# Two attention and two feed-forward layers: VectorE copies both single scores of a cycle, one exponential for the pair, another order of tokens in turned chunks

## The chip, the cores and the metric

The kernel runs on one core of one Trainium2 chip. The metric is the device time of one execution in microseconds (us). The engines are named as the profile names them: PE (TensorE, matmuls), DVE (VectorE), ACT (ScalarE), POOL (GpSimd) and SP (SyncE, which here only issues DMAs).

## The reference

Input x has 2048 tokens of D = 448 numbers. The same attention and the same feed-forward block are applied twice, in turn:

```python
def _A_ref(x, wq, wk, wv, wo):          # H = 16 heads of Dh = 28, one k and one v for all heads
    q = (x @ wq).reshape(B, S, H, Dh).transpose(0, 2, 1, 3)
    k = x @ wk
    v = x @ wv
    scores = jnp.einsum("bhqd,bkd->bhqk", q, k) * (Dh ** -0.5)
    p = _softmax(scores, axis=-1)
    o = jnp.einsum("bhqk,bkd->bhqd", p, v)
    return o.transpose(0, 2, 1, 3).reshape(B, S, H * Dh) @ wo
def _B_ref(x, w_gate, w_up, w_down):    # F = 1792
    return (_silu(x @ w_gate) * (x @ w_up)) @ w_down

x = x + _A_ref(_layernorm(x)); x = x + _B_ref(_layernorm(x))
x = x + _A_ref(_layernorm(x)); x = x + _B_ref(_layernorm(x))
```

All is float32. The kernel splits a float32 factor into a high and a low part and adds three products, so that PE can take the faster form of matmul; P-V alone is done in plain float32.

## The kernel before, in words

The tokens stand in four chunks of 512. The order of the instructions on each engine is the order in which the program text issues them.

**Attention (`scores`).** There are 16 groups, each of one chunk of queries and four heads. For a group the 2048 keys come in 16 tiles of 128, and a cycle (`cycle`, L610) takes two of these tiles: 16 / 2 = 8 cycles a group, 128 a layer. For each tile `tile_scores` (L592) makes four banks of scores, one a head: three lie side by side in a tile named three, the fourth, the single, in a bank of its own. In a cycle ACT makes four exponentials: of the first single out of its bank (L614), of the first three (L615), of the second three (L618), and of the second single (L619), which DVE has copied from its bank into SBUF (L617). Then PE does P-V of the cycle before (`pv`, L651) into the bank that held the first single, and DVE adds the result to the group's sum (L660). Small work of DVE, POOL and SP (`due`, `aside`) is issued behind that: the end of a group's normalisation, and the layer norm and turning of finished chunks. In the fifth cycle of some groups `outproj` (L577) multiplies a finished chunk by wo.

PE takes its work in this order: scores of two tiles for cycle m, P-V of cycle m - 1, scores for m + 1, and so on. There are eight banks: two times three, and the two of the singles, which change places from cycle to cycle. The second single of a cycle goes into the bank from which the sum of the P-V before was read.

**Turning.** Matmuls need a chunk with features on the partitions. Chunks 0 to 2 of each feed-forward layer are turned while attention runs: `turn_tile` (L266) transposes 128 tokens in blocks of 32x32 on DVE (L268) and sends them with four DMAs to a DRAM tensor (L271); later `rows3` (L130, L132) reads the whole chunk back as features by tokens, and `halved` splits it. For layer 1's attention `hand_over` (L844) makes the layer norm of a chunk as soon as the feed-forward layer has finished it, and PE turns it with 16 transposes (`flip`, L248); ACT (L254, L258) and DVE (L255, L264) take the result out of PSUM.

**Feed-forward (`unit`).** A unit is one chunk times 128 of the 1792 hidden columns. PE does the first half of gate and up (22 matmuls), one half of the unit before's down projection (12), the second half (20) and the other half of down (12). ACT reads one column of the banks ("seen", L325), for which the next half waits; then come Silu (L922), the product with up on DVE (L923), and the split into h high (ACT, L924) and low (DVE, L927). Two stage copies (L829) and POOL additions (L830) end a chunk. What `hand_over` puts into the list `soon` is issued at the end of a later unit; the number says how many units later. `project` (L298) is the q, k, v product for 112 + 16 columns of a chunk; `q` stores it to DRAM (qd, kt). When the queries of chunk 0 are stored, `fetch` (L444) loads them again, POOL casts them (L446), and `maxima` (L424) makes the shifts for the exponentials from them.

Of the kernel before, what the change touches and what calls it, by code (L numbers as in the profile page):

```python
# [55 lines left out]
def forward(  # L56
# [209 lines left out]
    def turn_tile(got, tb, raw, t):  # L266

        nc.vector.transpose(tb[:, t, :], got["x"][:, t, 0:D])  # L268
        to = raw.rearrange("(b d) (t g w) -> t g d b w", d=32, g=4, w=32)
        for g in range(4):  # L270
            nc.sync.dma_start(to[t, g], tb[32 * g : 32 * g + 32, t, :].rearrange("d (b w) -> d b w", w=32))  # L271
# [57 lines left out]
    class Attention:  # L329


        def __init__(self, layer):
            self.layer = layer
            self.X, self.norms, self.qd = {}, {}, {}
# [172 lines left out]
        def q(self, c, m):  # L507
            cs = slice(512 * c, 512 * c + 512)
            held, po = bank((3, 4, 5) if self.seen > len(self.order) - 4 else wide[-1], True)
# [9 lines left out]
            if not full and (c or not self.layer):  # L519
                if self.seen % 2 == 0:  # L520
                    self.two = wpool.tile([P, 2, 512], F32R, tag="wgh", name="q2", bufs=FG + 1)
                self.hi[m] = self.two[0:112, self.seen % 2, :]
                nc.scalar.copy(self.hi[m], po[0:112, :])
            nc.scalar.copy(raw, po)
# [7 lines left out]
            vt = vt.rearrange("p (t u d) -> p u t d", t=4, u=4)  # L532
# [21 lines left out]
        def scores(self, ff, xb):  # L554
            next(switch)
            inner = ExitStack()
            with tc.tile_pool(name=f"ow{self.layer}", bufs=1, side="right", reuse_waits="tile") as ow:
                wp = inner.enter_context(tc.tile_pool(name=f"at{self.layer}", bufs=1, reuse_waits="tile"))
                woh = ow.tile([P, NG, D], F32R, name="woh")
# [25 lines left out]
                def tile_scores(n, three, one):  # L585

                    i, kt = divmod(n, NT)
                    q, k, ks = qts[i % 3], keys[kt // 4], slice(P * (kt % 4), P * (kt % 4) + P)
                    for z, (kp, part) in enumerate(((0, 0), (1, 0), (0, 1))):
                        for j in range(4):  # L590
                            js = slice(32 * j, 32 * j + 32)
                            nc.tensor.matmul(  # L592
                                three[:, j, :] if j < 3 else one, k[js, kp, ks], q[js, part, :],
                                start=(z == 0), stop=(z == 2), tile_position=(32 * j, 0),
                            )
                    pt, pt1 = bufs[n % 4]
# [4 lines left out]
                bufs = [  # L601
                    (wp.tile([P, 3, 512], F32, name=f"pt{y}"), wp.tile([P, 512], F32, name=f"single{y}"))
                    for y in range(4)
                ]
# [5 lines left out]
                def cycle(m):  # L610

                    a, b = singles(m)
                    pt, pt1 = tile_scores(2 * m, threes[0], a)
                    es = [nc.scalar.activation(pt1, a, AF.Exp, scale=SCALE)]  # L614
                    es.append(nc.scalar.activation(pt, threes[0], AF.Exp, scale=SCALE))  # L615
                    pt, pt1 = tile_scores(2 * m + 1, threes[1], b)
                    copy = nc.vector.tensor_copy(pt1, b)  # L617
                    es.append(nc.scalar.activation(pt, threes[1], AF.Exp, scale=SCALE))  # L618
                    es.append(nc.scalar.activation(pt1, pt1, AF.Exp, scale=SCALE))  # L619
# [3 lines left out]
                    if m > 1:  # L623
                        tc.declare_no_dep(copy.ins, exps[m - 2][3], reason="P-V, which read it, waited for that")
# [20 lines left out]
                def pv(m, to):  # L645
# [18 lines left out]
                    if m + 1 in exps:  # L664
                        tc.declare_no_dep(f.ins, exps[m + 1][0], reason="P-V waited for the bank's exponential")
# [37 lines left out]
                def turns(c, got):  # L703

                    at_ = {}

                    def one(t):
                        if t == 0:
                            at_["tb"] = wp.tile([P, 4, D], F32, name="tb")
                        turn_tile(got, at_["tb"], ff.raw[c], t)  # L710
# [26 lines left out]
                for m in range(last):  # L737
# [13 lines left out]
                    cycle(m)  # L751
                    if m:
# [29 lines left out]
    class FeedForward:  # L782
# [61 lines left out]
        def hand_over(self, c):  # L844

            a = self.nxt
            fs, got = norm_steps(c)
# [3 lines left out]
            a.X[c] = xtile((xpool, self.x1p, self.xbp, self.xbp)[c])  # L851

            def ready():
                for f in fs[5:]:
                    f()
                if c > 1:
                    a.norms[c] = got

            if c == NC - 1:
                a.plan[8, 0] = [ready]  # L860
# [27 lines left out]
        def unit(self, gi, c, n):  # L888
# [33 lines left out]
            nc.scalar.activation(sg, pg[0], AF.Silu)  # L922
            nc.vector.tensor_tensor(sg, pg[1], sg, ALU.mult)  # L923
# [147 lines left out]
```

## Time and profile before

| | |
|---|---|
| median of 3 runs | 1992.53 us (1992.45 to 1994.26) |
| the profiled execution | 1995.44 us |
| its span, first to last instruction | 1993.7 us |
| mean granted TensorE clock | 0.997 |
| busy: PE / ACT / DVE / POOL | 1973.1 / 1276.1 / 782.7 / 559.9 us |
| attention of layer 0 and of layer 1 | about 69 to 577 us, and 1055 to 1561 us |
| longest waits: DVE for ACT's Silu (L923) | 503.5 us in 110 |
| POOL for ACT's stage copies (L830) | 498.1 us in 53 |
| PE's weight loads of scores for ACT's exponential (L615) | 187.6 us in 222 |

A busy time counts from start to modelled end, and matmuls overlap, so PE's share tells little of what bounds the kernel. The group of a line is a helper's where a helper issues it: L318 is every matmul of the feed-forward layer, L298 every one of the projections. In the order of time a row gives start, length, engine, line, operation, what it writes and reads, and in brackets the idle time of the engine ahead of it. In the chain of work that ended last a row gives start, length and what the chain ran through. "SPq" is SP issuing a DMA; the data moves afterwards.

### The profile page before, as it was taken

What the parts mean: (1) busy time and instruction counts of PE and PEld (TensorE: products, weight loads), DVE (VectorE), ACT (ScalarE), POOL (GpSimd) and SP (SyncE); (2) the same over time, 40 slices, a digit from 0 to 9 for tenths busy, and PEclk for the clock granted to TensorE, in tenths of its full rate; (3) what the DMA queues carried; (4) which work ended last, traced back from release to release, by engine and by line L of the source; (5) the groups of instructions that cost most, each with busy time, mean ns of one, the idle gap of its engine ahead of it and who ended that gap; (6) DMA issues with size and microseconds to landing.
All of it is one profiled execution on the core that took longest, in us unless ns stands there. A gap on an engine that the chain in (4) does not pass through costs nothing.

```text
span 1993.7 us, 43630 instructions
## 1 busy us (share of the span) xinstructions
PE 1973.1 (99%) x18517; PEld 1305.8 (65%) x18517; DVE 782.7 (39%) x1370; ACT 1276.1 (64%) x2140; POOL 559.9 (28%) x611
## 2 busy tenths in 40 slices
PE   8999999999999999999999999999999999999998
PEld 7544534445458999999884444444454689988886
DVE  6443343443534232322464444435444432222222
ACT  4799798997963333333348997979979433333332
POOL 4213123122214233333341221132231243233320
PEclk9999999999999999999999999999999999999999
DMA  5201011021120111100031010200212200011102
GB/s 156 61 23 33 17 30 44 17 51 32 39 62 22 31 32 31 32 18 25 22 95 40 26 30 12 62 12 22 51 32 62 53 17 27 21 31 32 32 1 76
DMA packets 126496, 75.50 MB, mean 38 GB/s; under 512 B 69688, under 2 KB 110008, under 8 KB 126296
## 3 DMA queue, kind: packets, MB, share of 16 engines
q1 hardware_dynamic: 124744, 71.46, 13.5%
q8 instruction: 146, 2.39, 0.5%
q10 hardware_dynamic: 1552, 1.20, 0.2%
q14 instruction: 54, 0.44, 0.1%
HBM read 54.01 MB, written 17.83 MB: 36 GB/s over the span
## 4 chain that ended last, share of the span: by engine, by line
PE 96%; DVE 1%; DMA 1%; ACT 1%; POOL 0%; issue 0%; ACTq 0%; SPq 0%; DVEq 0%; POOLq 0%
PE bank L318 40%; PE bank L651 25%; PE three L592 20%; PE bank L298 4%; PE bank L592 3%; PE three L577 2%; PE bank L577 2%; PE bank L248 1%; DMA wr<-in_A_wq_dram 0%; DMA qd<-stage 0%; DVE xn L230 0%; DMA xd<-xh 0%; DMA kt<-stage 0%; DVE xres L581 0%; PE bank L424 0%
## 5 line engine op out<-in xcount | busy, mean ns | idle before, releaser
L651 PE MATMUL bank<-pt,vsb 128*32 128x512 f32 x3072 | 491.9, 600 | 0.0
L651 PE MATMUL bank<-single,vsb 128*32 128x512 f32 x1024 | 488.6, 600 | 0.0
L592 PE MATMUL bank<-qstack,keys 32*128 32x512 f32 x1536 | 470.5, 424 | 2.2 <-DVE xres L581 1.7
L592 PE MATMUL three<-qstack,keys 32*128 32x512 f32 x4608 | 461.7, 425 | 3.6 <-ACT pt L615 2.4
L318 PE MATMUL bank<-xh,wgh 64*128 64x512 f32 x1728 | 446.4, 389 | 0.0
L592 PEld LDWEIGHTS three<-qstack,keys 32*128 32x128 f32 x4608 | 251.6, 183 | 297.0 <-ACT pt L615 187.6
L618 ACT ACTIVATE pt<-three 128x1536 f32<-128x1536 f32 x256 | 408.7, 1597 | 0.0
L615 ACT ACTIVATE pt<-three 128x1536 f32<-128x1536 f32 x256 | 405.3, 1583 | 2.6 <-DMA kt<-stage 2.6
L318 PE MATMUL bank<-xh,wgl 64*128 64x512 f32 x1404 | 368.5, 390 | 0.0
L318 PE MATMUL bank<-xl,wgh 64*128 64x512 f32 x1296 | 334.7, 389 | 0.0
L318 PE MATMUL bank<-wdh,h 64*128 64x448 f32 x1792 | 332.5, 364 | 1.5 <-ACT h L924 0.8
L923 DVE TENSOR_TENSOR sg<-bank,sg 128x512 f32<-128x512 f32 x112 | 77.5, 692 | 507.6 <-ACT sg L922 503.5
L318 PEld LDWEIGHTS bank<-xh,wgh 64*128 64x128 f32 x1728 | 263.0, 184 | 18.1 <-issue 1.6
L651 PEld LDWEIGHTS bank<-pt,vsb 128*32 128x32 f32 x3072 | 101.9, 109 | 261.2 <-issue 153.3
L830 POOL TENSOR_TENSOR xres<-stage,xres 128x448 f32<-128x448 f32 x108 | 127.2, 1197 | 498.3 <-ACT stage L829 498.1
L660 DVE TENSOR_TENSOR o<-bank,o 128x512 f32<-128x512 f32 x224 | 154.9, 692 | 277.7 <-PE bank L651 277.7
L617 DVE COPY single<-bank 128x512 f32<-128x512 f32 x256 | 177.0, 691 | 211.4 <-PE bank L592 205.0
L318 PEld LDWEIGHTS bank<-wdh,h 64*128 64x128 f32 x1792 | 244.5, 184 | 16.0 <-issue 2.3
L694 POOL TENSOR_TENSOR o<-o 128x512 f32<-128x512 f32 x32 | 41.3, 1290 | 740.2 <-DMA o<-rd 331.6
L592 PEld LDWEIGHTS bank<-qstack,keys 32*128 32x128 f32 x1536 | 243.8, 183 | 5.4 <-DVE xres L581 3.6
L325 ACT COPY seen<-bank 128x1 f32<-128x1 f32 x664 | 81.9, 163 | 255.0 <-PE bank L318 252.3
L614 ACT ACTIVATE single<-bank 128x512 f32<-128x512 f32 x256 | 187.8, 734 | 64.4 <-PE bank L592 64.4
(131 smaller groups left out, 2716.8 us busy)
## 6 DMA issues: line engine op xcount, KB each, us to landing
o<-rd SPq DMA_DIRECT2D x32, 256.0 KB
qd<-stage SPq DMA_DIRECT2D x32, 224.0 KB
qraw<-qd SPq DMA_DIRECT2D x128, 56.0 KB
wdr<-in_B_w_down_dram SPq DMA_DIRECT2D x28, 224.0 KB
xt<-tb SPq DMA_DIRECT2D x96, 56.0 KB
wr<-in_B_w_gate_dram SPq DMA_DIRECT2D x28, 192.0 KB
wr<-in_B_w_up_dram SPq DMA_DIRECT2D x28, 192.0 KB
xn<-xt SPq DMA_DIRECT2D x6, 768.0 KB
```

Of the source, the lines that this page charges most:

```text
L298: nc.tensor.matmul(po, a, b, start=(i == 0), stop=(i == len(seq) - 1))
L318: nc.tensor.matmul(po, a, b, start=start, stop=stop, skip_group_check=True)
L325: nc.scalar.copy(seen[:, i : i + 1], po[:, 0:1])
L577: nc.tensor.matmul(po[:, 0:D], a[:, g, ts_], b[:, g, :], start=(g + z == 0), stop=(g == NG - 1 and z == 2))
L592: nc.tensor.matmul(three[:, j, :] if j < 3 else one, k[js, kp, ks], q[js, part, :], start=(z == 0), stop=(z == 2), tile_position=(32 * j, 0),)
L614: es = [nc.scalar.activation(pt1, a, AF.Exp, scale=SCALE)]
L615: es.append(nc.scalar.activation(pt, threes[0], AF.Exp, scale=SCALE))
L617: copy = nc.vector.tensor_copy(pt1, b)
L618: es.append(nc.scalar.activation(pt, threes[1], AF.Exp, scale=SCALE))
L651: nc.tensor.matmul(to[32 * j : 32 * j + 32, :], vsb[:, n % NT, :], pts[n][j], start=(y == 0), stop=(y == 1), skip_group_check=True,)
L660: f = nc.vector.tensor_tensor(accs[i][:, 0, :], to, accs[i][:, 0, :], ALU.add)
L830: nc.gpsimd.tensor_tensor(r, s, r, ALU.add)
```

## The change

**In a cycle** both singles are copied by DVE into one tile of 128x1024 (two such tiles in turn), and after the two exponentials of three banks one exponential in place takes the pair. The first single is no longer read by ACT out of its bank. What `due` and `aside` hold for a cycle is issued between its scores and the P-V, not after it.

**Turned chunks** are collected in one tile and sent with four DMAs (rows of 512 bytes) where it were sixteen (rows of 128 bytes). In such a chunk token 128 t + 32 g + w stands in column 128 g + 32 t + w. The order is put right where the products leave PSUM: `natural` and `in_order` rearrange what Silu and the product with up read and write, and the copies of `q` in layer 1.

**The hand-over to layer 1** turns chunks 0 to 2 on DVE and through DRAM in place of PE; ACT and DVE split what comes back (`parts`). The copies for chunk 0 are issued two units after the chunk is finished, the two projections of chunk 0 three units after; chunk 2's copies behind the sixth projection. The copy of the last 64 features by POOL goes for these chunks.

```diff
-    def turn_tile(got, tb, raw, t):
-        nc.vector.transpose(tb[:, t, :], got["x"][:, t, 0:D])
-        to = raw.rearrange("(b d) (t g w) -> t g d b w", d=32, g=4, w=32)
+    def turn_tile(got, tb, t):
+        nc.vector.transpose(tb[:, :, 32 * t : 32 * t + 32], got["x"][:, t, 0:D].rearrange("p (b w) -> p b w", w=32))
+    def send(tb, raw):
+        to = raw.rearrange("(b d) (g n) -> g d b n", d=32, g=4)
         for g in range(4):
-            nc.sync.dma_start(to[t, g], tb[32 * g : 32 * g + 32, t, :].rearrange("d (b w) -> d b w", w=32))
+            nc.sync.dma_start(to[g], tb[32 * g : 32 * g + 32])
...
-                    a, b = singles(m)
-                    pt, pt1 = tile_scores(2 * m, threes[0], a)
-                    es = [nc.scalar.activation(pt1, a, AF.Exp, scale=SCALE)]
-                    es.append(nc.scalar.activation(pt, threes[0], AF.Exp, scale=SCALE))
-                    pt, pt1 = tile_scores(2 * m + 1, threes[1], b)
-                    copy = nc.vector.tensor_copy(pt1, b)
-                    es.append(nc.scalar.activation(pt, threes[1], AF.Exp, scale=SCALE))
-                    es.append(nc.scalar.activation(pt1, pt1, AF.Exp, scale=SCALE))
+                    es, copies, pair = [], [], pairs[m % 2]
+                    for y, one in enumerate(singles(m)):
+                        pt, pt1 = tile_scores(2 * m + y, threes[y], one)
+                        copies.append(nc.vector.tensor_copy(pt1, one))
+                        es.append(nc.scalar.activation(pt, threes[y], AF.Exp, scale=SCALE))
+                    es.append(nc.scalar.activation(pair, pair, AF.Exp, scale=SCALE))
...
                     cycle(m)
+                    if m in due:
+                        due.pop(m)()
+                    if m in aside:
+                        aside[m]()
                     if m:
                         pv(m - 1, singles(m)[0])
...
-                    if m in due:
-                        due.pop(m)()
-                    if m in aside:
-                        aside[m]()
...
+            raw = dram.tile([D, 512], F32, name=f"xt1_{c}")
+            def turn():
+                for f in fs[5:]:
+                    f()
...
+                for t in range(4):
+                    turn_tile(got, tb, t)
+                send(tb, raw)
+                a.X[c] = xtile(pool[c])
+                got["raw"] = pers.tile([P, 4, 512], F32, name="xn")
+                rows3(got["raw"], raw)
+            def parts():
+                halved(a.X[c], got["raw"], range(4), nc.scalar.copy, nc.vector.tensor_tensor)
-            self.soon.append([1, ready])
-            if c < 2:
-                self.mid[len(groups) - 1, c + 2, 0] = [lambda ks=ks: flip(got, a.X[c], ks) for ks in ((0, 1), (2, 3))]
-                self.soon.append([2, lambda: [a.project() for _ in range(2 - c)]])
+            self.soon.append([1, turn])
+            if c == 2:
+                a.plan[5, 1] = [parts]
+                return
+            self.soon.append([2, parts])
+            self.soon.append([3 - c, lambda: [a.project() for _ in range(2 - c)]])
...
-            nc.scalar.activation(sg, pg[0], AF.Silu)
-            nc.vector.tensor_tensor(sg, pg[1], sg, ALU.mult)
+            sq = c < NC - 1
+            nc.scalar.activation(in_order(sg, sq), natural(pg[0], sq), AF.Silu)
+            nc.vector.tensor_tensor(in_order(sg, sq), natural(pg[1], sq), in_order(sg, sq), ALU.mult)
```

More of the change, by code (lines that the diff above doesn't have):

```diff
@@ L333, in __init__ @@
             self.layer = layer
+            self.squares = (0, 1, 2) if layer else ()
             self.X, self.norms, self.qd = {}, {}, {}
@@ L600, in scores @@
                 exps, sums = {}, {}
[L601 to L604, printed above, removed]
+                bufs = [wp.tile([P, 3, 512], F32, name=f"pt{y}") for y in range(4)]
+                pairs = [wp.tile([P, 2, 512], F32, name=f"pair{y}") for y in range(2)]
                 def singles(m):
@@ L622, in cycle @@
                         tc.declare_no_dep(new, old, reason="P-V, which read the buffer, waited for the old one")
-                    if m > 1:
-                        tc.declare_no_dep(copy.ins, exps[m - 2][3], reason="P-V, which read it, waited for that")
+                    for f in copies if m > 1 else ():
+                        tc.declare_no_dep(f.ins, exps[m - 2][2], reason="P-V, which read it, waited for that")
                 def between_cycles(m):
@@ L703, in turns @@
                 def turns(c, got):
[L705 removed]
                     def one(t):
[L708 to L710 removed]
+                        turn_tile(got, tb, t)
+                        if t == 3:
+                            send(tb, ff.raw[c])
                     return [lambda t=t: one(t) for t in range(4)]
@@ L846, in hand_over @@
             a = self.nxt
-            fs, got = norm_steps(c)
+            fs, got = norm_steps(c, twice=c == NC - 1)
             for f in fs[:5]:
```

27 lines of the change are left out of this document (18 added, 9 removed).

## The prediction

> **What bounds the kernel now.** I read the page first: which engine is full, and in which slices.
>
> ```profile
> span 1993.7 us, 43630 instructions
> PE 1973.1 (99%) x18517; PEld 1305.8 (65%) x18517; DVE 782.7 (39%) x1370; ACT 1276.1 (64%) x2140; POOL 559.9 (28%) x611
> ACT  4799798997963333333348997979979433333332
> ```
>
> TensorE (PE) looks full, but in two stretches of some 500 us ScalarE (ACT) is at 9 tenths and over: the two attention stages. There a busy PE proves nothing, since ends of matmuls are modelled. So I look at one cycle, first in the chain of work that ended last, then in ACT's order of time.
>
> ```profile
> 91.23 1.91 PE bank L651 x16
> ...
> 135.45 1.92 PE bank L651 x16
> ```
>
> These are the first and last of 13 P-V pieces one cycle apart: 44.22 / 12 = 3.685 us a cycle.
>
> ```profile
> 402.98 0.75 ACT L614 ACTIVATE single<-bank 128x512 f32<-128x512 f32 x1
> 403.47 1.60 ACT L615 ACTIVATE pt<-three 128x1536 f32<-128x1536 f32 x1
> 404.80 1.61 ACT L618 ACTIVATE pt<-three 128x1536 f32<-128x1536 f32 x1
> 406.13 0.80 ACT L619 ACTIVATE single<-single 128x512 f32<-128x512 f32 x1
> 406.67 0.75 ACT L614 ACTIVATE single<-bank 128x512 f32<-128x512 f32 x1
> ```
>
> The starts lie 0.49, 1.33, 1.33 and 0.54 us apart, together 3.69, and each begins before the one ahead has ended: ACT has no gap, it is the bound. How far could the cycle fall if ACT were shorter? One early cycle, in which ACT still had slack, answers (PE and VectorE (DVE) in order of time):
>
> ```profile
> 80.26 0.63 PE L651 MATMUL bank<-pt,vsb 128*32 128x512 f32 x3
> 81.59 0.59 PE L651 MATMUL bank<-single,vsb 128*32 128x512 f32 x1
> 82.25 0.69 DVE L660 TENSOR_TENSOR o<-bank,o 128x512 f32<-128x512 f32 x1 [1.19 <-PE bank L651]
> 82.70 0.39 PE L592 MATMUL bank<-qstack,keys 32*128 32x512 f32 x1
> 83.00 0.49 PE L592 MATMUL bank<-qstack,keys 32*128 32x512 f32 x1
> 83.56 0.38 PE L592 MATMUL bank<-qstack,keys 32*128 32x512 f32 x1
> 83.88 0.63 PE L651 MATMUL bank<-pt,vsb 128*32 128x512 f32 x3
> 83.98 0.69 DVE L617 COPY single<-bank 128x512 f32<-128x512 f32 x1 [1.04 <-PE bank L592]
> ```
>
> P-V starts at 80.26 and its last matmul ends at 82.18; the sum follows 0.07 later and ends at 82.94; the single score of the second tile, which is written into the bank just summed, starts at 83.00; the next P-V at 83.88. That is a closed loop of 3.62 us, one sum in each cycle, and the change leaves it. So at most 0.07 us a cycle is to be had.
>
> **The change, part by part: the cycle.** The exponential of the first single (L614) goes; DVE copies both singles and one exponential of 128x1024 in SBUF ends the cycle. ACT: from 512 to 1536 columns the distance grows by 1.33 - 0.49 = 0.84, so 0.42 for 512 more, and the new one takes 0.54 + 0.42 = 0.96. ACT's cycle is 1.33 + 1.33 + 0.96 = 3.62. Bounds for the new exponential: 0.91 (0.49 + 0.42) and 1.03 (0.49 + 0.54, nothing saved); 0.96 lies nearest to the row in SBUF that it extends.
>
> In the Trainium skill, page "ScalarE: Activation LUTs", section "What ACT_TABLE_LOAD costs", an ACTIVATE with immediate scale and bias takes 186 ns plus 0.833 ns an element, and neighbours overlap by 93 ns. By it one instruction fewer saves 93 ns, and ACT's cycle would be 3.59; the rows (0.49 for 512, 1.33 for 1536) agree with that slope.
>
> DVE's second copy starts where L614 did. In the rows above the first single is written until 82.70 + 0.39 = 83.09; a copy starts 0.04 after its matmul (83.94 to 83.98) and takes 0.69, so it ends at 83.82 and P-V, which overwrites that bank, can start at 83.87: the place where the loop of the sum puts it anyway (83.88). P-V waits for the pair's exponential too, but one cycle later. Counted from the P-V at 80.26: first scores done at 2.83, ACT's two exponentials of three banks at 2.9 and 4.2, the pair's at 5.5 to some 6.75 (0.80 + 0.42, as L619 with 512 more); it is needed at 2 x 3.61 = 7.2. So three loops meet at 3.61 to 3.62, and I take 3.613 (the sum's loop by its unrounded starts), 0.072 less than now. Of 256 cycles some 245 are of this kind (the rest stand beside the output projections and the ends): 245 x 0.072 = **-17.6 us**. The ends give back: the last P-V has no scores ahead of it and waits for an exponential of 1.0 us that comes last.
>
> ```profile
> 572.80 4.22 PE bank L651 x32
> ```
>
> Now the last two P-Vs take 4.22 where two of 1.92 are work, a gap of 0.38; by the same phases (6.75 against 3.6 + 1.9) it becomes some 1.25: +0.9 in each layer, **+1.8 us**.
>
> Small work ahead of the sum: each cycle leaves DVE idle from the second copy's end (84.67) to the sum (85.87), 1.2 us.
>
> ```profile
> L217 DVE BATCH_NORM_STATS2 stats<-xres 128x6 f32<-128x448 f32 x64 | 38.8, 607 | 4.2 <-DMA xres<-in_A_x_dram 4.2
> L218 DVE BATCH_NORM_AGGREGATE mv<-stats 128x2 f32<-128x6 f32 x64 | 11.7, 182 | 2.2
> L268 DVE STREAM_TRANSPOSE tb<-xn 128x448 f32<-128x448 f32 x24 | 15.2, 635 | 0.0
> ```
>
> The largest pieces are 0.79 (607 + 182 ns) and 0.64, so they fit: 0. Without that cover each would delay a sum by its length; there are about 50 such cycles in a layer.
>
> **The hand-over to layer 1.** Chunks 0 to 2 are no longer turned by PE (48 transposes) but by DVE, through DRAM.
>
> ```profile
> 971.11 0.35 ACT L325 COPY seen<-bank 128x1 f32<-128x1 f32 x2 [1.63 <-PE bank L318]
> 971.94 0.76 PE bank L248 x5
> 972.71 1.43 PE bank L318 x12
> 974.14 1.02 PE bank L248 x8
> 975.16 3.74 PE bank L318 x32
> 1026.81 1.75 PE bank L248 x16
> ```
>
> In the chain PE's half unit is done at 971.1, and without the 1.43 of L318 the stretch to 975.16 is 2.6 us of transposes and waiting for xn. Twice that (chunk 1 looks alike) and 1.75: **-6.9 us**. But the way through DRAM puts a wait on ACT. In the changed order ACT's four copies out of the returned tile stand right behind the two stage copies of the unit that follows the turn, and ahead of the "seen" copies of the next unit, for which PE's second half waits. Before, two projections of layer 1 stood there and covered; they come one unit later now.
>
> ```profile
> 970.11 1.77 DVE L230 TENSOR_SCALAR xn<-xres,mv,rstd 128x448 f32<-128x448 f32 x4
> 972.31 1.07 ACT L254 CAST xh<-bank 128x512 fp32r<-128x512 f32 x2 [0.85 <-PE bank L248]
> 296.21 2.11 SPq L271 DMA_DIRECT2D xt<-tb  x4
> 299.74 0.39 SPq L130 DMA_DIRECT2D xn<-xt  x1
> 299.70:306.30 6.60, 6.60 (x76) 2.50 (x68) 3.10 (x9) 6.60 (x9) 0.00 (x0) 1.00 0.70 195
> 555.40:559.70 4.30, 4.30 (x52) 1.51 (x40) 2.15 (x7) 4.30 (x6) 0.00 (x0) 1.00 0.92 241
> ```
>
> xn is ready at 971.88, four transposes of 0.635 end at 974.4. Four sends of 57 KB take SyncE (SP) 3.53 us from the first issue to the read behind them (296.21 to 299.74). Now each is 229 KB, 0.92 MB in all; at 241 GB/s that is 3.8 us and, with 1 us to start, 4.8: the read is issued at about 979.2. Its 1.05 MB take 4.3 to 5.4 us (241 and 195 GB/s, last column of the windows), and three quarters, with which ACT can begin, are there near 983. Four copies 0.48 apart and the "seen" pair end near 985.3. Without transposes PE would have got there at 971.1 + 1.43 + 3.74 + 2.6 (22 matmuls at the 0.117 of L318 x32) + 1.43 = 980.3. So it waits **+5 us** (0 if both trips run in half the time, 8 with sends as slow as 195 GB/s and a late last quarter). Chunk 1's trip has the two projections in between: about 0.
>
> In the Trainium skill, "DMA: Bandwidth & Descriptors", section "Anatomy of one DMA — SWDGE (gpsimd) path", a transfer costs 2.0 us and its bytes at 436 GB/s; by that the two trips take 4.1 and 4.4 us, PE would wait some 1.5 us less at each of the two places, and the total would be 3 us lower. That page speaks of another queue; these rows are slower.
>
> Chunk 2's trip stands on SP ahead of the stores and loads (qd, wrq) from which the first maxima of layer 1 are made:
>
> ```profile
> 1015.53 0.31 SPq L525 DMA_DIRECT2D qd<-stage  x1
> 1016.02 2.07 SPq L444 DMA_DIRECT2D wrq<-qd  x4
> 1022.93 2.02 POOL L446 CAST q<-wrq 112x1024 fp32r<-112x1024 f32 x2
> 1025.88 0.93 PE bank L424 x4
> ```
>
> Its sends go out at about 1017.7, the read at 1022.2, so qd and wrq are issued at 1023.8 to 1026.3 instead of 1015.5 to 1018.1. Their 0.9 MB land behind the read at 1028 to 1030, GpSimd (POOL) casts for 1.0 us more, and the maxima (L424), due at 1025.9, start their second half near 1030.5: **+4.5 us** (0 to 8). ACT's wait for chunk 2 lies under the same time. Elsewhere the other order of tokens changes only the patterns of copies of the same size, on engines that are not late there: 0.
>
> **Sum**, on the profiled execution of 1995.44 us (span 1993.7): -17.6 + 1.8 - 6.9 + 5 + 4.5 = -13.2, so 1982.2; on the median of the runs, 1992.53, which lies 2.9 lower, **1979.3 us**.
>
> **Rivals.** (1) The hand-over is hidden: the trips are fast enough or PE finds other work. For it: no row here shows an engine late for an xn out of DRAM. Against: those were asked for many cycles ahead, these one unit. -17.6 + 1.8 - 6.9 gives 1969.8. (2) ACT alone sets the cycle, and the loop of the sum has slack that one cycle doesn't show: what ACT saves comes off whole. With the new exponential at 0.94, between 0.91 and 0.96 of the rows, 0.49 + 0.54 - 0.94 = 0.09 comes off 3.685: 245 x 0.09 = 22, with +2.6 from the hand-over and +1.8 from the ends 1975. (The rule of the Trainium skill quoted above, from "ScalarE: Activation LUTs", points the same way: 3.59 for ACT's cycle.) (3) The change does not shorten the cycle: the exponential over 1024 in SBUF takes the 1.03 of the two, ACT stays the bound at 3.685. Then -6.9 + 1.8 + 9.5 = +4.4: 1996.9. Against it: the slope of 0.42 for 512. (4) Slower: DVE's operations stretch. P-V now waits for a DVE copy on top of a DVE sum; if twice as many copies beside POOL and ACT push each from 0.69 to 0.80, the loop is 3.72, 245 x 0.038 = +9, and with +2.6 and +1.8 it is 2006. It decides from 0.76 a DVE operation.
>
> ```profile
> L617 DVE COPY single<-bank 128x512 f32<-128x512 f32 x256 | 177.0, 691 | 211.4 <-PE bank L592 205.0 <-DMA kt<-stage 3.9 <-PE three L592 2.4
> L927 DVE TENSOR_TENSOR h<-sg,h 128x512 fp32r<-128x512 f32 x112 | 95.8, 855 | 61.3 <-ACT h L924 61.3
> ```
>
> For it: L927, out of SBUF, averages 855 ns where 690 would do. Against it: 256 copies out of PSUM average 691.
>
> **How the numbers follow.** Forecast 0.54, (1) 0.16, (2) 0.10, (3) 0.11, (4) 0.09. A measurement of this kernel tells about 0.2% (4 us) from no change. The forecast's own range is 1970 to 1990 (the waits at the hand-over from 0 to 16 us in all, a cycle from 3.61 to 3.64). 1968 to 1993 takes in (1) and (2) and leaves out (3) and (4), 0.20. Faster: 0.52 + 0.16 + 0.10 = 0.78; within 0.2%: 0.08 (0.02 and half of (3)); slower 0.14.
>
> **What would show it.** P-V to P-V at 3.61 to 3.63 in the chain, with small gaps on ACT ahead of the three-bank exponentials; DVE's two copies still at 0.69; starts of the exponential of 128x1024 and its successor 0.94 to 0.97 apart. No L248 for chunks 0 to 2; a PE gap of about 5 us behind an ACT copy that waits for xn, and one of about 4.5 ahead of the maxima. Cycles of 3.68 with ACT full, or copies above 0.76, would prove it wrong; so would a hand-over without those gaps.

## The result, and the profile after

The changed kernel takes **2008.6 us** (median of 4 runs, 2006.66 to 2011.9), against 1993.39 for the kernel before (4 runs on the same chip): ratio 1.0077, 95% interval 1.006 to 1.0094. The prediction was 1979.3 and faster; it was slower by 15 us. The profiled execution took 2011.9 us. In what follows, line numbers (L629) are those of the kernel of the run shown, and a run is named by its label (e1 for e1_cycle_only). The page of the changed kernel:

```profile
span 2010.2 us, 43798 instructions
PE 1964.7 (98%) x18469; PEld 1339.7 (67%) x18469; DVE 967.1 (48%) x1638; ACT 1267.9 (63%) x1884; POOL 557.0 (28%) x599
L629 DVE COPY pair<-bank 128x512 f32<-128x512 f32 x512 | 353.8, 691 | 100.0 <-PE bank L608 71.2
```

The copies stayed at 691 ns although there are twice as many. The span grew by 16.5 us. Split at the first and the last but one P-V of each layer, the attention of layer 0 takes 497.5 us as before and that of layer 1 495.8 (495.9 before); the stretch from the last but one P-V of layer 0 to the first of layer 1 grew by 17.7 us (488.1 to 505.8); the start is 1.9 shorter, the end 0.7 longer. So the loss lies between the layers, and attention hides something: its cycles did get shorter.

**The cycle.** PE and then DVE in order of time, in the changed kernel:

```profile
362.28 0.63 PE L663 MATMUL bank<-pt,vsb 128*32 128x512 f32 x3
...
402.42 0.63 PE L663 MATMUL bank<-pt,vsb 128*32 128x512 f32 x3
...
404.28 0.50 PE L608 MATMUL bank<-qstack,keys 32*128 32x512 f32 x1
...
404.85 0.39 PE L608 MATMUL bank<-qstack,keys 32*128 32x512 f32 x1
...
406.07 0.63 PE L663 MATMUL bank<-pt,vsb 128*32 128x512 f32 x3
```

```profile
404.41 0.69 DVE L672 TENSOR_TENSOR o<-bank,o 128x512 f32<-128x512 f32 x1 [0.67 <-PE bank L663]
405.32 0.69 DVE L629 COPY pair<-bank 128x512 f32<-128x512 f32 x1 [0.22 <-PE bank L608]
406.16 0.69 DVE L629 COPY pair<-bank 128x512 f32<-128x512 f32 x1 [0.15 <-PE bank L608]
```

From 362.28 to 406.07 are 12 cycles: 3.649 us each (3.685 before, 3.613 predicted). Follow the copy (L629) of the first single: its last matmul (L608) ends at 404.85 + 0.39 = 405.24, the copy starts at 405.32 and ends at 406.01, P-V starts at 406.07. Over 223 cycles the medians from one P-V (L663) to the next are 2.827 to the end of that matmul, 0.073 to the copy, 0.692 for the copy and 0.056 to P-V: together 3.648. The prediction had the same chain with 0.04 where 0.073 is.

**Long cycles.** Eight cycles take 3.84 to 5.96 us, 9.0 us more than eight ordinary ones. Six of them stand right behind the four sends of a turned chunk. Of the other two, one (5.19) follows the longest, with the granted clock at 0.5 for 3.4 us from 554.6 on; in the other (3.84) an operation of the layer norm, L230, stands ahead of the sum and takes 1.59 us where its median is 0.51. The longest, DVE, SP and PE in order of time:

```profile
548.99 0.69 DVE L629 COPY pair<-bank 128x512 f32<-128x512 f32 x1 [0.20 <-PE bank L608]
552.30 0.18 DVE L692 TENSOR_SCALAR under<-rs 128x16 f32<-128x16 f32 x1 [2.62 <-DMA rs<-o]
...
553.18 0.63 DVE L672 TENSOR_TENSOR o<-bank,o 128x512 f32<-128x512 f32 x1
```

```profile
542.91 3.02 SPq L274 DMA_DIRECT2D xt<-tb  x4
545.99 3.50 SPq L686 DMA_DIRECT2D rs<-o  x4
```

```profile
553.86 0.50 PE L608 MATMUL bank<-qstack,keys 32*128 32x512 f32 x1 [1.93 <-DVE o L672]
```

The row sums (rs) are asked for at 545.99 to 549.49, right behind 0.92 MB of sends on the same queue. (Before, the same bytes went out in four batches, one a cycle.) DVE's operation on them (L692, part of `due`) now stands ahead of the sum (L672). It waits until 552.30, the sum with it, and PE stands for 1.93 us, since the second tile's single goes into the bank of that sum. In the whole trace DVE stands 9.5 us in front of L692 for that DMA, in six cycles.

**The hand-over.** The chain of work that ended last, then one row of DVE and three of PE in order of time (L331 is the feed-forward layer, L311 the projections, L438 the maxima):

```profile
974.73 4.33 DMA xt<-xh
979.20 5.21 DMA xn<-xt
984.43 0.94 ACT xh L291 x2
...
986.77 5.96 PE bank L331 x31
...
1005.66 5.07 DMA xn<-xt
...
1013.42 0.13 ACT seen L338 x2
1013.59 3.80 PE bank L331 x32
...
1031.18 0.37 SPq L458
...
1031.61 5.42 DMA wrq<-qd
...
1037.14 1.10 POOL q L460
...
1040.12 1.22 PE bank L438 x2
1041.34 12.33 PE bank L311 x44
```

```profile
1020.51 2.22 DVE L268 STREAM_TRANSPOSE xh<-xn 128x448 f32<-128x448 f32 x4
```

```profile
986.77 0.80 PE L331 MATMUL bank<-xh,wgh 64*128 64x512 f32 x2 [8.13 <-ACT seen L338]
...
1024.92 0.51 PE L311 MATMUL bank<-xh,wh 128*128 128x512 f32 x1 [1.26 <-DVE xres L834]
...
1040.12 1.22 PE L438 MATMUL bank<-q,kdiag 112*128 112x512 f32 x2 [6.96 <-POOL q L460]
```

PE waits 8.13 us for chunk 0 (5 predicted), 1.43 for chunk 1 (0 predicted), and 6.96 at the maxima (4.5 predicted). A fourth wait, 1.26 us, is new as well: DVE's four transposes of chunk 2 stand ahead of L834, which frees the bank that PE needs. And what follows a long gap is slow: 31 matmuls of L331 take 5.96 at 986.77, and 32 take 3.80 at 1013.59. In the windows the PE clock (third column from the right) shows why:

```profile
981.30:991.50 10.20, 4.73 (x22) 3.79 (x24) 2.59 (x4) 2.67 (x11) 0.00 (x0) 0.50 0.29 92
...
1040.10:1046.00 5.90, 5.88 (x14) 4.64 (x15) 3.43 (x7) 0.00 (x0) 1.18 (x5) 0.50 0.42 145
```

At both places the granted clock is halved for 10.2 us from within the gap on. That costs 2.2 us behind each (5.96 against 3.74 to 3.80; the 44 matmuls 12.3 against some 10.1).

The account between the layers: -6.9 (no transposes) + 8.1 + 1.4 + 1.3 + 7.0 (the four waits) + 2 x 2.2 (the halved clock) + 0.7 (the longer end of attention) + 0.7 (two gaps of 0.9 just ahead of layer 1's first P-V; they were 0.5 each before) = +16.7 of the 17.7. In the attention stages 245 x 0.037 = -9.1 and the long cycles' +9.0 cancel.

### The profile page after: what moved, and what is told of

Same layout as the page of the kernel before. It is cut to its first block, busy times and chain, and to the rows that moved or that the text cites. A ratio compares the mean times of both kernels' runs of the same rounds, so it can differ in the third digit from the quotient of the medians.

```text
span 2010.2 us, 43798 instructions
## 1 busy us (share of the span) xinstructions
PE 1964.7 (98%) x18469; PEld 1339.7 (67%) x18469; DVE 967.1 (48%) x1638; ACT 1267.9 (63%) x1884; POOL 557.0 (28%) x599
## 3 DMA queue, kind: packets, MB, share of 16 engines
q1 hardware_dynamic: 98584, 77.36, 13.7%
## 4 chain that ended last, share of the span: by engine, by line
PE 46%; DMA 2%; DVE 1%; SPq 1%; issue 0%; ACT 0%; POOL 0%; DVEq 0%; ACTq 0%; POOLq 0%
PE bank L331 20%; PE bank L663 11%; PE three L608 7%; PE bank L608 4%; PE bank L311 2%; PE three L593 1%; PE bank L593 1%; DMA xn<-xt 1%; SPq L686 0%; DMA xt<-xh 0%; DMA rs<-o 0%; SPq L274 0%; DMA qd<-stage 0%; DMA wrq<-qd 0%; DVE pair L629 0%
## 5 line engine op out<-in xcount | busy, mean ns | idle before, releaser
L630 ACT ACTIVATE pt<-three 128x1536 f32<-128x1536 f32 x512 | 716.4, 1454 | 72.7 <-PE three L608 67.9
L663 PE MATMUL bank<-pt,vsb 128*32 128x512 f32 x3072 | 492.3, 600 | 2.0 <-DVE pair L629 1.5
L663 PE MATMUL bank<-pair,vsb 128*32 128x512 f32 x1024 | 488.9, 600 | 0.5 <-ACT pair L631 0.5
L608 PE MATMUL bank<-qstack,keys 32*128 32x512 f32 x1536 | 471.2, 425 | 7.1 <-DVE o L672 5.4
L331 PE MATMUL bank<-xh,wgh 64*128 64x512 f32 x1728 | 449.1, 391 | 9.6 <-ACT seen L338 9.6
L608 PE MATMUL three<-qstack,keys 32*128 32x512 f32 x4608 | 431.3, 408 | 2.0 <-ACT stage L539 1.1
L608 PEld LDWEIGHTS three<-qstack,keys 32*128 32x128 f32 x4608 | 261.1, 183 | 231.9 <-issue 194.2
L629 DVE COPY pair<-bank 128x512 f32<-128x512 f32 x512 | 353.8, 691 | 100.0 <-PE bank L608 71.2
L331 PE MATMUL bank<-xh,wgl 64*128 64x512 f32 x1404 | 370.3, 391 | 0.0
L331 PE MATMUL bank<-xl,wgh 64*128 64x512 f32 x1296 | 336.6, 391 | 0.0
L331 PE MATMUL bank<-wdh,h 64*128 64x448 f32 x1792 | 333.3, 364 | 1.5 <-ACT h L952 0.8
L331 PEld LDWEIGHTS bank<-xh,wgh 64*128 64x128 f32 x1728 | 265.0, 185 | 27.0 <-ACT seen L338 10.3
L608 PEld LDWEIGHTS bank<-qstack,keys 32*128 32x128 f32 x1536 | 243.8, 183 | 44.7 <-DVE o L672 8.3
L631 ACT ACTIVATE pair<-pair 128x1024 f32<-128x1024 f32 x256 | 273.0, 1066 | 0.0
L663 PEld LDWEIGHTS bank<-pt,vsb 128*32 128x32 f32 x3072 | 101.9, 109 | 253.4 <-issue 153.9
L331 PEld LDWEIGHTS bank<-wdh,h 64*128 64x128 f32 x1792 | 246.5, 184 | 14.5 <-issue 2.0
L672 DVE TENSOR_TENSOR o<-bank,o 128x512 f32<-128x512 f32 x224 | 154.5, 690 | 208.0 <-PE bank L663 208.0
L331 PEld LDWEIGHTS bank<-xh,wgl 64*128 64x128 f32 x1404 | 218.2, 185 | 13.9
```

The lines of the kernel that those rows point to most:

```text
L331: nc.tensor.matmul(po, a, b, start=start, stop=stop, skip_group_check=True)
L608: nc.tensor.matmul(three[:, j, :] if j < 3 else one, k[js, kp, ks], q[js, part, :], start=(z == 0), stop=(z == 2), tile_position=(32 * j, 0),)
L629: copies.append(nc.vector.tensor_copy(pt1, one))
L630: es.append(nc.scalar.activation(pt, threes[y], AF.Exp, scale=SCALE))
L631: es.append(nc.scalar.activation(pair, pair, AF.Exp, scale=SCALE))
L663: nc.tensor.matmul(to[32 * j : 32 * j + 32, :], vsb[:, n % NT, :], pts[n][j], start=(y == 0), stop=(y == 1), skip_group_check=True,)
```

## The experiments

My theory: three separate losses (long cycles 9, gaps at the hand-over 16, halved clock 4.5) stand against a gain in the cycle of half the size predicted. The rivals are these: the new cycle itself is worth nothing or harms; the long cycles belong to the new cycle's order and not to the sends; the hand-over's gaps are one loss shifted from place to place.

| run | time, us | ratio to before, 95% interval | P-V to P-V, us |
|---|---|---|---|
| the change | 2008.6 | 1.0077 (1.006 to 1.0094) | 3.648 |
| e1_cycle_only | 1986.58 | 0.9964 (0.9952 to 0.9977) | 3.648 |
| e2_pe_turns | 1991.87 | 0.9994 (0.9984 to 1.0003) | 3.65 |
| e3_due_later | 2001.39 | 1.0043 (1.0026 to 1.0059) | 3.65 |
| e4_copies_later | 1996.22 | 1.0017 (1.0007 to 1.0027) | 3.65 |
| e5_two_mended | 1985.4 | 0.9967 (0.9954 to 0.9979) | 3.647 |
| e6_half_copy | 2001.8 | 1.0049 (1.0033 to 1.0066) | 3.631 |
| e7_two_chunks | 1982.61 | 0.9951 (0.9934 to 0.9967) | 3.648 |
| e8_work_behind | 2037.06 | 1.0225 (1.0208 to 1.0242) | 3.648, 98 others |
| e9_single_first | 1980.1 | 0.9931 (0.9918 to 0.9945) | 3.632 |
| e10_filler | 2008.94 | 1.0082 (1.0066 to 1.0098) | 3.647 |

The kernel before had medians of 1992.3 to 1992.5 beside these runs.

**e1: the kernel before with the cycle alone** (pairs, one exponential for both, small work ahead of the sum). Its sends and its hand-over are the old ones.

```diff
-                    es = [nc.scalar.activation(pt1, a, AF.Exp, scale=SCALE)]
...
+                        copies.append(nc.vector.tensor_copy(pt1, one))
...
+                    es.append(nc.scalar.activation(pair, pair, AF.Exp, scale=SCALE))
```

> The kernel before with the change to the cycle alone (both singles copied by DVE, one exponential for the pair, small work ahead of the sum); turning and hand-over as before. Theory (the cycle is shorter by 0.037 us, bound by DVE's copy of the first single on the way to P-V; the long cycles of the changed kernel come from its bigger sends): P-V to P-V 3.648 us, none of the cycles of 4.3 to 6.0 us, 1993 - 9 = 1984 to 1986 us. Rival A (the long cycles come from small work that now stands ahead of the sum, whatever is sent): the same eight long cycles, about 9 us, so 1992 to 1994. Rival B (the cycle itself loses): above 1996.

The chain of this kernel:

```profile
397.16 1.87 PE bank L647 x16
...
411.76 1.87 PE bank L647 x16
```

Four cycles in 14.60 us, 3.65 each, and no long one. The new cycle is a gain of its own, and small work ahead of the sum costs next to nothing beside the old sends. The span fell by 6.4 us: the two attention stages are 8.1 shorter (9.1 by the ordinary cycles, less a few of 3.70 to 3.76), their ends give back 1.3, and the rest of the kernel 0.4.

**e2: the changed kernel with PE's turns at the hand-over** (the old `hand_over`).

```diff
-            self.squares = (0, 1, 2) if layer else ()
+            self.squares = ()
...
-            self.soon.append([1, turn])
+            self.soon.append([1, ready])
```

> The changed kernel with the hand-over to layer 1 as before (PE turns chunks 0 to 2). Theory (the waits at the hand-over cost 18 us of idle PE and some 4 us of a slower clock behind them, and save 7): 2008.6 - 16 = 1991 to 1994, no PE gap over 1 us between 960 and 1055 us, clock at full there; the long cycles in attention stay. Rival (the loss is in attention or in the reordered feed-forward copies): 2004 or more.

16.7 us come back. No gap over 1 us is left between the layers except 1.59 just ahead of the first P-V, and the clock stays whole from 960 to 1050 us. The long cycles stay (4.2 to 5.8 us) and eat the cycle's gain: the time is that of the kernel before.

**e3: the row sums asked for one cycle later** (`due` at m + 4, and the output projection in the seventh cycle of a group, where the changed kernel and the one before have it in the sixth).

```diff
-                        due[m + 3] = post(i)
+                        due[m + 4] = post(i)
...
-                    if not todo or u != 5:
+                    if not todo or u != 6:
```

> The changed kernel with the end of a group's normalisation one cycle later (four cycles behind its sums and not three), and the output projection in the seventh cycle of a group and not the sixth. Theory (in eight cycles DVE stands at the row sums, which arrive late behind the sends of a turned chunk, with the sum and so PE queued behind): the long cycles shrink or go, 2008.6 - 5 to - 9, so 1999 to 2004. Rival (the long cycles come from the DVE transposes or from POOL): they stay, 2007 to 2010.

DVE in order of time at the place of the longest cycle:

```profile
549.73 0.16 DVE L692 TENSOR_SCALAR under<-rs 128x16 f32<-128x16 f32 x1
...
551.03 0.69 DVE L672 TENSOR_TENSOR o<-bank,o 128x512 f32<-128x512 f32 x1 [0.34 <-PE bank L663]
```

L692 waits for nothing, and the sum waits for its P-V again. 7.2 us of the 9.0 come back; two cycles of 4.3 and some of 3.87 stay. The gaps at the hand-over stay (8.23 and 6.40).

**e4: the changed kernel with ACT's copies of what comes back, and the projections, a unit later.**

```diff
-            self.soon.append([2, parts])
-            self.soon.append([3 - c, lambda: [a.project() for _ in range(2 - c)]])
+            self.soon.append([3, parts])
+            self.soon.append([4 - c if c == 0 else 3, lambda: [a.project() for _ in range(2 - c)]])
```

> The changed kernel with ACT's copies of the returned chunks 0 and 1 one unit later, and the projections behind them. Theory (ACT stands in order at the copies until the chunk is back from DRAM, and PE at the column that ACT reads behind them): the PE gaps of 8.1 and 1.4 us go, and with the first the slow clock behind it; the one ahead of the maxima (7 us) stays: 2008.6 - 10 to - 13, so 1995 to 1999. Rival (PE waits for something else, such as DVE or the loads): the gaps stay, 2006 to 2010.

PE in order of time:

```profile
985.26 0.50 PE L331 MATMUL bank<-xh,wgh 64*128 64x512 f32 x2 [0.95 <-ACT seen L338]
...
1027.94 0.79 PE L438 MATMUL bank<-q,kdiag 112*128 112x512 f32 x1 [6.86 <-POOL q L460]
```

The first gap falls from 8.13 to 0.95, the second is gone, and behind them the clock is whole; the wait behind DVE's transposes of chunk 2 grows to 2.21, and the one at the maxima stays. So the wait at the maxima is not the first one passed on.

**e5: e2 and e3 together.**

```diff
-                        due[m + 3] = post(i)
+                        due[m + 4] = post(i)
...
-            self.soon.append([1, turn])
+            self.soon.append([1, ready])
```

> The changed kernel with two parts taken back: chunks 0 to 2 are turned by TensorE again at the hand-over, and the row sums are asked for one cycle later (the output projection one cycle later too). My theory: the hand-over (8.1 + 1.4 + 7.0 us of gaps and about 4.5 us of halved clock) and the long cycles (9 us) are separate losses and add up. TensorE's turns alone gave 1991.9, the later row sums alone took 7.2 us from 2008.6; so 1991.9 - 7.2 = about 1985. Rival: they overlap, or the later row sums only move the wait (to the output projection); then 1989 to 1992.

The time is 1985.4 us. The two losses add up: 16.7 + 7.2 = 23.9, and 23.2 was measured. With token order and bundled sends kept, the stretch between the layers is 489.3 us, against 489.2 in e1, which has neither: the other order of tokens costs nothing there.

**e6: e1, and of each first single only half is copied.** The other half of those columns holds no scores; it begins as zero (a memset on POOL). Against e1:

```diff
-                        copies.append(nc.vector.tensor_copy(pt1, one))
+                        copies.append(nc.vector.tensor_copy(*((pt1, one) if y else (pt1[:, 0:256], one[:, 0:256]))))
```

> The kernel before with the cycle change alone, and of each first single VectorE copies only half (256 of 512 columns); the other half of those columns in the pair is never filled with scores. It is a measurement of the loop: the first copy takes about 0.35 us less (0.34 for 0.69). My theory: the loop P-V, scores of the second... first single's last matmul, copy, P-V sets the cycle at 3.648; without 0.35 us of it the next loop takes over: ScalarE's three exponentials (1.33 + 1.33 + 0.947 to 0.972 = 3.61 to 3.63) or the loop of the sum (3.61). So the cycle falls to 3.60 to 3.63 and the time by 5 to 12 us, to 1975 to 1982. Rival 1: the loop of the sum, or ScalarE, sets 3.648 already; then the cycle stays and the time is 1986 to 1987. Rival 2: the copy alone sets the cycle and nothing stands close behind: 3.35 or less, 75 us lower.

The chain (the two P-Vs lie two cycles apart), one row of DVE, and the start of the attention stage in the chain:

```profile
397.46 1.85 PE bank L649 x16
...
404.73 1.85 PE bank L649 x16
```

```profile
403.94 0.42 DVE L615 COPY pair<-bank 128x256 f32<-128x256 f32 x1 [0.23 <-PE bank L592]
```

```profile
75.18 0.90 POOL pair L604
...
76.58 2.08 PE bank L424 x4
```

The copy is 0.27 shorter and the cycle falls from 3.648 to 3.631: the copy's loop set it, and the next limit is 0.017 behind. P-V now starts 0.31 behind the copy. The loop of the sum fits as that limit: PE starts the second single 0.055 behind the end of the sum, and P-V 0.950 behind it (medians). But in the early cycle of the prediction that last step was 0.93, and why it is longer here is not shown. ACT is close behind: its starts lie 1.347 and 1.330 apart, and 0.947 at the least, 3.624 in all; its first exponential still waits for the scores, 0.05 behind them. The two attention stages are 5.1 shorter than in e1. The time rose all the same, to 2001.8, against my 1975 to 1982. It is not the cycle's: the added memsets stand on POOL ahead of the copies and the maxima, PE waits 10.6 us at the start of each layer's attention, and the clock is halved for 13.7 us from within each wait on.

**e7: e3 and e4 together, and chunk 2 turned by PE.**

```diff
+                if c == 2:
+                    self.soon.append([1, ready])
```

> The changed kernel with three edits: chunk 2 is turned by TensorE (chunks 0 and 1 still through DRAM), ScalarE's copies of what came back are issued a unit later, and the row sums are asked for one cycle later. My theory: the 7.0 us gap ahead of the maxima came from chunk 2's trip, which stands on SyncE and in its queues ahead of the loads for the maxima; without it that gap falls under 1.5 us, the first gap to about 1, and the clock is not halved there. From 1996.2 (copies later) come off 7.2 (row sums) and 6 to 8 (maxima and their slow stretch): 1981 to 1984. Rival: the maxima's load is late for another reason (the projections come later, or the trips of chunks 0 and 1): the gap stays at 5 to 7 us and the time is 1988 to 1990.

The time is 1982.6 us. The maxima in the chain:

```profile
1005.54 7.79 PE bank L311 x33
1013.34 0.93 PE bank L438 x4
1014.27 1.75 PE bank L248 x16
```

They follow at once; the gap is gone, so it was chunk 2's trip ahead of their loads on SP and in its queue. The stretch between the layers is 484.6, 4.7 shorter than with PE's turns (e5). For two chunks the prediction's rows gave 6.9 - 1.75 = 5.2. So the way through DRAM is worth nearly what it was said to be, once nobody waits for it. The 1.26 us wait behind DVE's transposes of chunk 2 is gone too.

**e8: the changed kernel with the small work behind the sum again.**

```diff
-                    if m in due:
-                        due.pop(m)()
-                    if m in aside:
-                        aside[m]()
                     if m:
                         pv(m - 1, singles(m)[0])
...
+                    if m in due:
+                        due.pop(m)()
+                    if m in aside:
+                        aside[m]()
```

> The changed kernel with the small work of due and aside issued behind the P-V and its sum again, as before; all else is kept. My theory: the eight long cycles come from VectorE's row-sum operation that waits for its DMA behind the bigger sends, and holds the sum queued behind it; behind the sum it would hold the next copies instead, which are due about a sum (0.7) and 0.3 us later, so the eight shrink by about 1 us each (-7 to -9 us); but now each piece of small work (0.2 to 0.8 us, in some 50 cycles of a layer) delays the first copy of the next cycle, which has about 0.2 us of slack, +0.2 to +0.5 us in each of some 60 to 100 cycles, +15 to +30. Together 2013 to 2030. Rival: the small work fits either way (the place of the work is of no account beside the sends): 2000 to 2002. Rival 2: the place of the work has nothing to do with the long cycles: they stay and the time is 2008 or more.

DVE in order of time:

```profile
430.82 0.69 DVE L672 TENSOR_TENSOR o<-bank,o 128x512 f32<-128x512 f32 x1 [1.19 <-PE bank L663]
431.43 0.16 DVE L692 TENSOR_SCALAR under<-rs 128x16 f32<-128x16 f32 x1
...
432.30 1.22 DVE L629 COPY pair<-bank 128x512 f32<-128x512 f32 x2
434.97 0.69 DVE L672 TENSOR_TENSOR o<-bank,o 128x512 f32<-128x512 f32 x1 [1.46 <-PE bank L663]
```

The row sums' operations are done at 432.3, the copies wait for them, and sum to sum is 4.15 us. Some 98 of the P-V to P-V distances are not the ordinary one (15 in the changed kernel), and the time is 2037, above my 2013 to 2030. With two copies a cycle, small work belongs ahead of the sum; what must not stand there is an operation that waits for a late transfer.

**e9: e7, and in the first tile of a cycle the matmuls of the single ahead of the three's.**

```diff
-                        for j in range(4):
+                        for j in range(4) if n % 2 else (3, 0, 1, 2):
```

> The kernel of the mended hand-over (chunks 0 and 1 through DRAM, copies and row sums later; 1982.6) with one edit: in the first tile of a cycle the matmuls of the single score are issued ahead of those of the three. The copy that P-V waits for can start earlier, by up to three matmuls (some 0.2 us), and nothing is added. My theory: the loop through that copy sets the cycle at 3.648, and with it shorter the loop of the sum does, 3.631 as in the run with the half copy: 245 x 0.017 = -4.2, so about 1978.5, P-V to P-V at 3.63. Rival 1: the single's last matmul ends no earlier (the four row groups of TensorE run side by side, whatever their order): 3.648 and 1982.6. Rival 2: the exponential of the first three, which now gets its last matmul later, makes ScalarE late, and the cycle grows to 3.68 or more: 1990.

PE and DVE in order of time:

```profile
401.98 0.63 PE L663 MATMUL bank<-pt,vsb 128*32 128x512 f32 x3
...
404.40 0.39 PE L608 MATMUL bank<-qstack,keys 32*128 32x512 f32 x1
...
409.24 0.63 PE L663 MATMUL bank<-pt,vsb 128*32 128x512 f32 x3
```

```profile
404.83 0.69 DVE L629 COPY pair<-bank 128x512 f32<-128x512 f32 x1 [0.17 <-PE three L608]
```

Two cycles in 7.26: 3.63, as in e6, and **1980.1 us** (2.5 less than e7, as the two attention stages of the traces have it; 4.2 expected, of which six longer cycles beside the output projections, 14.49 in place of 14.31, take 1.1). It is the fastest of all, ahead of both kernels. But my reason was half wrong: the single's last matmul ends hardly earlier (2.816 behind P-V against 2.827). What changed is the step from there to the copy, 0.037 in place of 0.073 (404.79 to 404.83 here).

**e10: the changed kernel with 24 matmuls in the gap ahead of the maxima,** whose result is overwritten.

```diff
+            if self.layer and c == 0:
+                for _ in range(24):
+                    nc.tensor.matmul(pm, kd[0:112, TURN[0], :], self.hi[TURN[0]], start=True, stop=True)
```

> The changed kernel with one edit: ahead of the first maxima of layer 1, where TensorE stands idle for 7.0 us, 24 matmuls are added whose result is overwritten (24 x 0.28 = 6.6 us of work in the gap). Nothing else changes, and the maxima still wait for the same load. My theory: it is the idle time that halves the granted clock afterwards. With the gap filled, the clock stays at 1.0 behind it, the 44 matmuls that follow take 10.3 in place of 12.5, and the time falls by about 2.3 us, to 2006.3; the clock behind the first gap (8.1 us, left alone) is still halved for 7 to 10 us. Rival: the clock falls for another reason (the stage, the DMA traffic of the hand-over, the kind of matmul): it is halved at both places, and the time stays at 2008.6 or rises by what the added matmuls take.

The windows, and the row behind the gap in PE's order of time:

```profile
1027.70:1033.40 5.70, 5.70 (x26) 4.64 (x25) 1.78 (x3) 2.67 (x5) 0.97 (x1) 1.00 1.03 296
...
1035.30:1046.00 10.70, 10.69 (x47) 8.87 (x48) 7.06 (x12) 3.32 (x6) 6.05 (x13) 1.00 0.47 142
```

```profile
1035.31 0.50 PE L441 MATMUL bank<-q,kdiag 112*128 112x512 f32 x1 [1.44 <-POOL q L463]
```

A gap of 1.44 is left, the clock stays at 1.00 and the 44 matmuls take 10.2 in place of 12.3 to 12.5; behind the first gap, left alone (8.24), it is halved for 10.2 us. So idle time of PE brings the halved clock. The median, 2008.94, shows nothing of the 2.3 us that I expected. The runs lie between 2006.5 and 2011.4, which would hide it; and in the traces only 0.8 of it is left at the first P-V of layer 1 (505.0 us between the layers against 505.8), since a gap of 1.61 and 3.4 us of halved clock follow just ahead of it.

## Why the prediction was wrong, point by point

1. **The cycle, -17.6.** The mechanism was right, the size half: 245 x 0.037 = -9.1. The mis-sized term is the start of the first copy, "0.04 after its matmul", taken from a copy behind the second single. Behind the first single it is 0.073, and the copy's loop is 3.648. The 3.613 for the loop of the sum was too low as well: it comes from one early cycle, and where the copy no longer holds P-V the cycle is 3.631 (e6, e9). The exponential of the pair was right: the distance behind it is 0.97, and 0.957 in e6 and 0.955 in e9, where the cycle asks for it (0.96 predicted).
2. **Small work ahead of the sum, 0. This step failed**, by +9.0. Only lengths were weighed (0.79 into 1.2), not what the operations wait for; `due`'s operation on the row sums waits for a DMA, and the change itself had put 0.92 MB at once in front of it. e1 shows the place alone is harmless, e3 that a cycle more takes 7.2 back. Some 1.5 of the 9.0 is the halved clock behind the longest wait.
3. **Ends, +1.8:** 572.78 to 577.02 before and 568.64 to 573.55 in e1 from the last but one P-V on: +0.67 in each layer, +1.3.
4. **Transposes gone, -6.9:** nearly borne out by e7 (-4.7 of 5.2 for two chunks).
5. **Chunk 0's wait, +5: 8.1.** The trip takes 972.96 to 984.43, 11.5 us where the terms made 8.6, up to three quarters of the read: the way to the read is 6.2 (4.8 predicted, with 1 us of it to start that no row was given for), the read 5.2 to its first use (ACT began behind the whole read, not behind three quarters). That the read was issued at the very time predicted, 979.2, is luck: the sends began 1.4 earlier than forecast. **Chunk 1's, 0: 1.4.** The same way; the two projections did not cover it all.
6. **The maxima, +4.5: 7.0.** The mechanism was right (e7), and the delay came out near: wrq is issued 15.2 us later than before (1031.18 against 1016.02), PE is 6.6 later at the maxima (1032.52 against 1025.88), and the difference, 8.5, is near the 8.3 predicted. That is luck in part: the sends went out at 1022.76, 1.5 before the forecast time moved by PE's 6.6, and wrq came 8.4 behind them where 6.6 was forecast. The mis-sized term is the way from that issue to the end of POOL's cast. The prediction gave it 6.2 (1024.3 to 1030.5); it takes 8.9 (1031.18 to 1040.07), and it took 8.9 before as well (1016.02 to 1022.93 + 2.02), with 0.9 to spare: two rows that stood in the prediction. 8.5 - 0.9 is 7.6, and 7.0 after the two matmuls that PE does first.
7. **Not in the sum: the halved clock,** 2 x 2.2, of which e10 shows that the idle time brings it; **and PE's wait for DVE behind the transposes of chunk 2,** 1.3, which is not there in e7.

The forecast of the hand-over, +2.6, thus became about +15, and 1 and 2 together turned -17.6 into nothing. None of the rivals took place: copies stayed at 691 ns (4), the cycle did fall (3), the hand-over was not hidden (1), ACT did not set the cycle alone (2). The slower side that came was not the one that the prediction priced. The order of tokens at 0 was right (e5 against e1).

What stays open: some 1.0 us of the stretch between the layers, and what sets the 3.631 of e6 and e9 to the last hundredth.

## What to carry to other kernels

When small work is moved ahead of an operation that the critical path needs, list what each piece waits for, not only how long it runs: a wait for a DMA holds everything queued behind it, and the same change may have put more bytes in front of that DMA. A round trip through DRAM is cheap if its result is used a stage later (e4, e7) and dear if it stands one unit ahead of its reader or in a queue ahead of someone else's load. Price an idle PE at more than the gap: here each of the two long ones cost 2.2 us more.

## What the runs showed of the hardware that was not expected

**The clock behind a gap.** In the twelve profiles PE gaps of 6.4 to 8.2 us go with a granted clock of 0.5 for 6.8 or 10.2 us, two gaps of 10.6 and 10.7 with 13.7; gaps of 1.5 to 2.8 with none, 3.4 or once 6.8. The lengths are multiples of 3.4 us, but for a last stretch that the end of each run cuts off. In the Trainium skill, "TensorE: Matmul & The Clock Gate", Part 1, an idle PE falls to half its clock after an idle window of about 3.4 us and is whole again after about 3.4 us of work. The trace agrees with the half and with the step of 3.4; the stretches behind long gaps are two to four such steps, since they begin within the gap. Gaps of 1.5 to 2.8 that bring one are shorter than the idle window that the Trainium skill gives; here the runs decide.

**The step from a matmul to its reader.** A copy starts 0.073 us behind its matmul where another matmul has just ended 8 ns ahead of it on the three (2.819 and 2.827 behind P-V), and 0.037 behind it in e9, where the single's matmul ends first (2.816 and 2.824). These ends are modelled, so the sum is surer than its parts: the copy starts 2.853 behind P-V in place of 2.900. In the Trainium skill, "TensorE: Matmul & The Clock Gate", "The cost: per-tile semaphore tail", it is said that the increments which matmuls make at their end are made one after the other, some 26 ns each. That fits a copy which waits for the second of two; the runs show the two distances, not the cause. The shorter step took 0.016 us off the median cycle, and 2.5 us off the run.
